# A planned attention and two-MoE kernel: GpSimd's elementwise work kept clear of its maxima, lower parts on VectorE, and q transfers issued closer together

## The chip, the cores and the metric

The kernel runs on one core of a Trainium2 chip. The metric is the device time of one execution, in microseconds. The engines are named as the profile names them: PE (TensorE; PEld its weight loads), DVE (VectorE), ACT (ScalarE), POOL (GpSimd), SP (SyncE, whose queue issues almost every transfer).

## What is computed

The reference, cut to what matters (batch 8, 8 heads, 576 positions, head size 64; all float32):

```
q_s = softmax(q, axis=-1)                      # over the 64 features
k_s = softmax(k, axis=2)                       # over the 576 positions
attn = q_s @ (k_s^T @ v)                       # per batch and head
x  = attn as [4608 tokens, 512]
x  = (silu(x @ w_gate) * (x @ w_val)) @ w_out              # d_ff 1536
out = max(x @ w1, x @ w2, x @ w3) @ w_out2                 # d_ff 768
```

## The kernel before

**Tiles and stages.** The 4608 tokens are nine blocks of 512. Each float32 operand of a product is split into a higher part, rounded to float32r, and a lower part, the rest; each product is three matmuls (high by high, high by low, low by high). Blocks 0, 1 and 2 are stages of their own. Blocks 3 and 4, 5 and 6, 7 and 8 are handled as **pairs**: the two blocks are the halves of a Strassen-Winograd scheme with seven products in place of eight (`wino_unit`, operands `b11`, `t1`, `t3`, `t2`, `b21`, `b22`, `t4`). In the trace the first pair fills about 560 to 910 us, the second 910 to 1240, the third the rest.

**Factors in the first pair.** In the pairs' products the weights' side needs seven factors for each piece of a weight. Three are the weights' own quarters; the other four are sums made earlier and kept in memory. In the first pair these four are read again (`twos_load`, line 626), split (`wino_hi`, line 634, the higher part on ACT; `wino_lo`, line 638, the lower part as sum minus higher part) and stored for the later pairs (`wino_store`, line 647). There are 84 such lower parts. `make_job` (line 1196 on) plans them. Later pairs only read the factors (line 653).

**Attention for later blocks** runs between the products as three chains of steps. The k chain (`k_steps`) loads k, takes the maximum over positions on DVE, then over partitions on POOL (`k_max_all`, line 195: `partition_all_reduce`), subtracts it (`k_sub`, lines 204 and 209), takes the exponential on ACT (line 218) and multiplies with v on PE (line 270). Two q chains (`q_steps`) each handle one half (four heads) of a block's q: loads of q (line 156, eight or sixteen transfers a half), maximum, subtraction (line 237), exponential (243), sum, multiplication by the reciprocal (256), transpose (410), split (414, 418) and the product with k and v (433 to 435, output `px`). One q chain, called `own`, has the second half of the heads and buffers of its own (`qown`). Six maxima on POOL are taken during pairs: four in the first pair, two in the second.

**What sets the order.** Nothing is scheduled by hand or by the framework. A planner written in the kernel walks a list of products and keeps for each engine a list of planned busy stretches with fixed costs. `gap` finds the first free stretch, `do` books it, `best` books whichever engine would end first, and `at` puts the instruction into a heap by planned time. Each engine then runs its instructions in the order of planned time, and what waits for what follows from the data. So a change of one cost or one booking moves work between engines and reorders everything behind it. GpSimd takes elementwise work only in pairs (`alone` is false there). The planner books a maximum as 1.4 us on POOL, an elementwise half tile on POOL as 0.85 us (`HALF`), and knows no time to go from one to the other:

```
            elif e == "B":
                ch["t"] = best(ch["t"], {"D": dur, "G": 2.0 * dur}, fn)
            ...
            else:
                ch["t"] = do(e[0], ch["t"], dur, fn)
```

In the built program POOL has an instruction of its own, shown as `ISA` without tiles, wherever it goes from an elementwise operation to a maximum or back. All transfers of a load step are planned at multiples of a spacing, 1.8 us for q.

Of the kernel before, what the change touches and what calls it, by code (L numbers as in the profile page):

```python
# [21 lines left out]
def linear_attention_moe_moe_kernel(  # L22
# [119 lines left out]
    def q_loads(t, j, hf):  # L142
        hs = slice(hf * HH, (hf + 1) * HH)
        cut = min(D * j, TB)
        todo = []
        for s0, s1 in ((0, cut), (cut, TB)):
            if s0 == s1:
                continue
            b, s = divmod(j * TB + s0, S)
            a = q[b, hs, s:s + s1 - s0, :].rearrange("(g u) (n p) (e i) -> u e g p n i", u=2, p=32, e=2)  # L150
            for u in range(2):
                for e in range(2):
                    p = 64 * u + 32 * e
                    for g in range(HP):
                        todo.append((slice(p, p + 32), g, slice(s0 // 32, s1 // 32), a[u, e, g]))
        return [lambda p=p, g=g, n=n, i=i: nc.sync.dma_start(out=t["qp"][p, g, n], in_=i) for p, g, n, i in todo]  # L156
# [263 lines left out]
    def x_mm(c, j, hf, g, tag):  # L420
        cut = min(D * j, TB)
        if cut == 0 or cut == TB:
            segs = [(0, TB, min(j, B - 1))]
        elif cut <= 256:
            segs = [(0, 256, j - 1), (cut, TB, j)]
        else:
            segs = [(256, TB, j), (0, cut, j - 1)]
        pg = hf * HP + g
        px = ps.tile([128, TB], F32, tag=tag, name="px")
        for a, e, b in segs:  # L430
            hi, lo = kvhi[b % 3][:, pg, :], kvlo[b % 3][:, pg, :]
            qhi, qlo = c["qt"][0][:, a:e], c["qt"][1][:, a:e]
            nc.tensor.matmul(out=px[:, a:e], lhsT=hi, rhs=qhi, start=True, stop=False)  # L433
            nc.tensor.matmul(out=px[:, a:e], lhsT=hi, rhs=qlo, start=False, stop=False)  # L434
            nc.tensor.matmul(out=px[:, a:e], lhsT=lo, rhs=qhi, start=False, stop=True)
        c["px"] = px
# [324 lines left out]
    HALF = {"A": 0.42, "D": 0.43, "G": 0.85}  # L761
    ENG = {"D": nc.vector, "G": nc.gpsimd, "A": None}
    DVE_LATE = 1.0
    KV_WAIT = 3.0
    G_FIRST = False
    LATER = {3: (1, "P", 0), 4: (2, "O", 0)}
# [15 lines left out]
    def at(t, fn, *a):  # L782
        heapq.heappush(events, (t, next(count), fn, a))
# [21 lines left out]
    def best(t, cost, fn, *a, engines="DG", by=0.0):  # L805

        if G_FIRST and not alone[0] and gap("G", t, cost["G"])[0] + cost["G"] < by:
            return do("G", t, cost["G"], fn, *a, nc.gpsimd)
        if alone[0]:
            engines = engines.replace("G", "")  # L810
        e = min(engines, key=lambda e: gap(e, t, cost[e])[0] + cost[e] + (0.4 if e == "G" else 0.0))
        return do(e, t, cost[e], fn, *a, ENG[e])
# [109 lines left out]
    def advance(ch):  # L922
        off = 0.45 * (ch is chains[1]) / 1.8
        while ch["steps"] and ch["steps"][0][0] != "P" and (ch["t"] <= clock[0] + LOOK[len(marks) - 1] or ch.get("bank")):
            e, dur, fn = ch["steps"][0]
            if e == "gate":
                if fn not in gates:
                    return
                ch["t"] = max(ch["t"], gates[fn])
            elif e == "there":  # L930
                there[fn] = ch["t"]
            elif e == "bank":
                bank_free[ch["bank"]] = max(bank_free.get(ch["bank"], 0.0), ch["t"])
                ch["bank"] = None
            elif e == "wait":
                ch["t"] += dur
            elif e == "open":
                gates[fn] = ch["t"]
            elif e == "load":
                t = max(ch["t"], ch.get("last", 0.0))  # L940
                for a in fn[1]:
                    t = (math.ceil(t / dur - off) + off) * dur
                    t = max(t + 0.01, sync(t, a))
                ch["last"] = t
                ch["loaded", fn[0]] = t + 4.5
            elif e == "loaded":
                ch["t"] = max(ch["t"], ch["loaded", fn])
            elif e == "B":
                ch["t"] = best(ch["t"], {"D": dur, "G": 2.0 * dur}, fn)
            elif e in ("D+", "D="):  # L950
                t, ch["i"] = take(ch["t"])
                ch["t"] = do("D", t, dur, fn, ch["i"])
            else:
                ch["t"] = do(e[0], ch["t"], dur, fn)
            if e in ("D-", "D="):
                drop(ch["i"], ch["t"])
            if DEBUG:
                log.append((round(clock[0], 1), chains.index(ch), e, round(ch["t"], 1)))
            ch["steps"].pop(0)
# [56 lines left out]
    def q_steps(runs, ts, direct, gate, own=False, free_q=False):  # L1016

        steps = []

        def load(n):  # L1020
            return "load", 1.8, (n, q_loads(ts[n % len(ts)], *runs[n]))

        for n, (j, hf) in enumerate(runs):
            c, t = {"own": own, "q": int(own)}, ts[n % len(ts)]
            if j in LATER:
                steps.append(("gate", 0.0, ("later", j)))
            if not direct:
                if n == 0:
                    if own:
                        steps.append(("gate", 0.0, gate))  # L1030
                    steps.append(load(0))
                    if own and len(runs) > 1:
                        steps.append(load(1))
                steps.append(("loaded", 0.0, n))
            steps += [
                ("D", 1.22, lambda c=c, t=t: q_max(t, c)), ("D", 0.95, lambda c=c, t=t: q_max_all(t, c)),
                ("B", 1.22, lambda e, c=c, t=t: q_sub(t, c, e)), ("A", 0.65 + 1.3 * direct, lambda c=c, t=t: q_exp(t, c, 0)),
                ("A", 0.65, lambda c=c, t=t: q_exp(t, c, 1)), ("D", 1.22, lambda c=c, t=t: q_sum(t, c)),
                ("D", 1.3, lambda c=c, t=t: q_sum_all(t, c)), ("B", 1.22, lambda e, c=c, t=t: q_mul(t, c, e)),
            ]  # L1040
            for g in range(HP):
                pg = hf * HP + g
                if g == 0 and not direct and not own and n + 1 < len(runs):
                    steps += [load(n + 1)] if free_q else [("gate", 0.0, ("k done",)), load(n + 1)]
                steps += [
                    ("D+", 0.7, lambda i, c=c, t=t, g=g: q_t(t, c, g, i)), ("A", 0.62, lambda c=c: q_t_hi(c)),
                    ("D-", 0.69, lambda c=c: q_t_lo(c)),
                ]
                if g == 0:
                    steps += [("gate", 0.0, ("taken", 2) if j == 4 else gate), ("gate", 0.0, ("kv", min(j, B - 1), hf))]  # L1050
                steps.append(("P", 0.75, lambda bank, c=c, j=j, hf=hf, g=g: x_mm(c, j, hf, g, bank)))
                if direct:
                    steps += [
                        ("A", 0.6, lambda c=c, j=j, pg=pg: x_hi(c["px"], j, pg)),
                        ("D", 0.69, lambda c=c, j=j, pg=pg: x_lo(c["px"], j, pg)), ("bank", 0.0, None),
                    ]
                    if pg % 2:
                        steps.append(("there", 0.0, ("op", f"b{pg // 2 + 1}1")))
                else:
                    steps += [("A", 0.6, lambda c=c, j=j, pg=pg: x_plain_copy(c["px"], j, pg)), ("bank", 0.0, None)]  # L1060
            if own and n + 2 < len(runs):
                steps.append(load(n + 2))
            if not direct:
                steps.append(("open", 0.0, ("x", j, hf)))
        return steps
# [132 lines left out]
    def make_job(use, key, k):  # L1198
        m = [k in t for t in TWOS].index(True)
        if ("two", key, m) not in have or not left("wA"):  # L1200
            return False
        t, o, ks = have["two", key, m]
        t, w = acquire("wA", max(t, use - 9.0))
        t = do("A", t, HALF["A"], wino_hi, key, k, w)
        t = there[key + (k,)] = best(t, HALF, wino_lo, key, k, by=use - 1.5)
        have["w", key + (k,)] = w, sync(max(use, t) + 1.5, wino_store, key, k)
        ks.discard(k)
        have["two", key, m] = max(t, have["two", key, m][0]), o, ks
        if not ks:
            release("or", o, have.pop(("two", key, m))[0])  # L1210
        return True
# [646 lines left out]
```

## Time and profile before

| what | value |
|---|---|
| median of 3 runs | 1563.69 us (1563.63 to 1568.78) |
| the profiled execution, its own time | 1565.22 us |
| its span (first to last instruction) | 1563.2 us |
| mean granted TensorE clock | 0.986 |
| busy: PE, DVE, ACT, POOL | 95%, 66%, 44%, 6% of the span |
| DMA engines | 71% of the span in the main queue |

A span is cut into instructions with the idle time before them and what released them. An engine's instructions run in order, so one that waits holds up all behind it. PE's busy time hides little: its matmuls start about 0.23 us apart when nothing holds them, and what the kernel can lose or gain is the time in which PE waits, and the stretches in which its granted clock is 0.5 in place of 1.0.

### The profile page before, as it was taken

How to read it: one execution, taken by the hardware profiler on the slowest of the kernel's cores; microseconds unless marked ns; L12 is line 12 of the kernel's file. 1: busy time of each engine (PE TensorE's matmuls, PEld its weight loads, DVE VectorE, ACT ScalarE, POOL GpSimd, SP SyncE). 2: the span in 40 equal slices, each digit the busy share in tenths (PEclk: the TensorE clock that was granted, in tenths of full speed). 3: DMA queues.
4: the chain of work that ended last, by engine and by line, in shares of the span. 5: the costliest groups of instructions: out<-in, count | busy, mean ns of one | idle time of the engine just before them, and what ended most of it. 6: DMA issues, size and time to landing. Idle time of an engine off the chain costs nothing.

```text
span 1563.2 us, 20625 instructions
## 1 busy us (share of the span) xinstructions
PE 1480.0 (95%) x6946; PEld 1201.1 (77%) x6946; DVE 1032.7 (66%) x1787; ACT 682.1 (44%) x1184; POOL 100.6 (6%) x86
## 2 busy tenths in 40 slices
PE   3888899999999999989999989999999999999999
PEld 2666687888778887877778877888778788887787
DVE  7879986767777677664478874564587844445553
ACT  3778765544546445544343344233322332224112
POOL 1000000000000001010022130000100300001000
PEclk9999899999999999999999999999999999999999
DMA  7798785974798798877478767774676576646664
GB/s 188 201 318 286 225 245 175 264 229 137 220 291 262 274 317 259 261 223 240 165 211 251 244 211 213 200 205 140 226 205 177 188 228 188 191 152 212 199 193 158
DMA packets 302024, 342.71 MB, mean 219 GB/s; under 512 B 157536, under 2 KB 181088, under 8 KB 301920
## 3 DMA queue, kind: packets, MB, share of 16 engines
q1 hardware_dynamic: 297120, 340.22, 71.2%
q10 hardware_dynamic: 4800, 1.18, 0.4%
q8 instruction: 56, 0.92, 0.2%
q14 instruction: 48, 0.39, 0.1%
HBM read 257.16 MB, written 84.15 MB: 218 GB/s over the span
## 4 chain that ended last, share of the span: by engine, by line
PE 76%; DVE 11%; DMA 6%; issue 3%; ACT 3%; SPq 1%; POOL 0%; DVEq 0%; ACTq 0%
PE pb L668 51%; PE pacc L684 15%; PE pb L684 8%; DMA v_sb<-in_v_dram 1%; PE pkv L270 1%; DMA plain<-raw_V 1%; DVE stage L543 1%; DVE tall L738 1%; DVE hlo L723 1%; DVE wall L567 1%; DMA raw_O<-plain 1%; SPq L156 1%; PE px L434 1%; DMA out_dram<-tall 1%; PE px L433 1%
## 5 line engine op out<-in xcount | busy, mean ns | idle before, releaser
L738 DVE TENSOR_TENSOR tall<-tall,pb 128x512 f32<-128x512 f32 x234 | 159.4, 683 | 195.1 <-PE pb L668 182.8
L668 PE MATMUL pb<-b11h,wall 128*128 128x512 f32 x756 | 267.1, 394 | 8.1 <-ACT s L704 4.6
L668 PE MATMUL pb<-b21h,wall 128*128 128x512 f32 x756 | 263.0, 390 | 0.0
L684 PE MATMUL pacc<-hhi,ow 128*128 128x512 f32 x576 | 191.8, 396 | 7.3 <-ACT hhi L719 6.0
L668 PEld LDWEIGHTS pb<-b11h,wall 128*128 128x128 f32 x756 | 142.3, 189 | 42.4 <-ACT s L704 5.9
L668 PEld LDWEIGHTS pb<-b21h,wall 128*128 128x128 f32 x756 | 141.9, 188 | 30.0 <-ACT tall L728 0.4
L728 ACT COPY tall<-pb 128x512 f32<-128x512 f32 x113 | 66.3, 587 | 203.6 <-PE pb L668 202.7
L668 PE MATMUL pb<-b11l,wall 128*128 128x512 f32 x378 | 147.9, 391 | 0.5 <-DVE b11l L455 0.5
L668 PE MATMUL pb<-b21l,wall 128*128 128x512 f32 x378 | 147.4, 390 | 0.4 <-DVE b21l L455 0.4
L684 PEld LDWEIGHTS pacc<-hhi,ow 128*128 128x128 f32 x576 | 110.0, 191 | 33.3 <-ACT hhi L719 8.6
L719 ACT CAST hhi<-tall 128x512 fp32r<-128x512 f32 x108 | 66.5, 617 | 139.0 <-DVE tall L713 103.6
L684 PE MATMUL pacc<-hlo,ow 128*128 128x512 f32 x288 | 114.7, 398 | 6.6 <-DVE hlo L723 6.6
L567 DVE TENSOR_TENSOR wall<-plain,wall 128x512 fp32r<-128x512 f32 x126 | 86.8, 692 | 43.8 <-ACT wall L564 36.7
L723 DVE TENSOR_TENSOR hlo<-tall,hhi 128x512 fp32r<-128x512 f32 x102 | 71.2, 698 | 52.3 <-ACT hhi L719 51.5
L564 ACT CAST wall<-plain 128x512 fp32r<-128x512 f32 x126 | 77.0, 617 | 64.3 <-DMA plain<-raw_G 14.7
L668 PE MATMUL pb<-b22h,wall 128*128 128x512 f32 x252 | 90.3, 399 | 7.0 <-POOL wall L638 6.0
L684 PE MATMUL pb<-hhi,ow 128*128 128x512 f32 x288 | 91.1, 391 | 1.1 <-DMA ow<-parts_O 0.9
L684 PE MATMUL pacc<-ow,hhi 128*128 128x512 f32 x288 | 89.3, 390 | 2.6 <-DVE ow L584 2.6
L668 PE MATMUL pb<-t4h,wall 128*128 128x512 f32 x252 | 88.7, 393 | 1.9 <-issue 1.9
L668 PE MATMUL pb<-t3h,wall 128*128 128x512 f32 x252 | 88.4, 391 | 2.1 <-DVE tall L738 1.2
L668 PE MATMUL pb<-t1h,wall 128*128 128x512 f32 x252 | 88.8, 393 | 0.0
L668 PE MATMUL pb<-t2h,wall 128*128 128x512 f32 x252 | 88.1, 390 | 0.0
(231 smaller groups left out, 2761.8 us busy)
## 6 DMA issues: line engine op xcount, KB each, us to landing
ow<-parts_O SPq DMA_DIRECT2D x77, 512.0 KB, 4.8
wall<-wino_W SPq DMA_DIRECT2D x153, 256.0 KB, 3.1
wall<-wino_G SPq DMA_DIRECT2D x102, 256.0 KB, 3.1
wall<-wino_V SPq DMA_DIRECT2D x102, 256.0 KB, 3.3
ow<-parts_P SPq DMA_DIRECT2D x32, 512.0 KB, 5.1
wino_W<-wall SPq DMA_DIRECT2D x63, 256.0 KB, 4.0
wino_G<-wall SPq DMA_DIRECT2D x42, 256.0 KB, 3.8
wino_V<-wall SPq DMA_DIRECT2D x42, 256.0 KB, 4.3
```

The lines of the kernel that those rows point to most:

```text
L156: return [lambda p=p, g=g, n=n, i=i: nc.sync.dma_start(out=t["qp"][p, g, n], in_=i) for p, g, n, i in todo]
L270: nc.tensor.matmul(out=c["pkv"][u * D:(u + 1) * D, g, :], lhsT=lhsT, rhs=rhs, start=i == 0, stop=i == R,)
L433: nc.tensor.matmul(out=px[:, a:e], lhsT=hi, rhs=qhi, start=True, stop=False)
L434: nc.tensor.matmul(out=px[:, a:e], lhsT=hi, rhs=qlo, start=False, stop=False)
L564: nc.scalar.copy(out=wall[:, i:i + 2, 0], in_=plain[kind, f].rearrange("p (a n) -> p a n", a=2))
L567: eng.tensor_tensor(out=wall[:, i:i + 2, 1], in0=plain[kind, f].rearrange("p (a n) -> p a n", a=2), in1=wall[:, i:i + 2, 0], op=ALU.subtract,)
L668: nc.tensor.matmul(out=banks[bank], lhsT=a, rhs=b, start=start and n == 0, stop=stop and n == 5, skip_group_check=True,)
L684: nc.tensor.matmul(out=banks[bank], lhsT=lhsT, rhs=rhs, start=first and n == 0, stop=last and n == 2)
L719: nc.scalar.copy(out=hid[key][0], in_=st["h", key[1], key[2], key[3]])
L723: eng.tensor_tensor(out=lo, in0=st.pop(("h", key[1], key[2], key[3])), in1=hi, op=ALU.subtract)
L728: nc.scalar.copy(out=tall[:, i], in_=banks[bank])
L738: eng.tensor_tensor(out=out_, in0=tall[:, x], in1=banks[bank] if isinstance(bank, str) else tall[:, bank], op=ALU.add)
```

## The change

Three edits, all in the planner:

- A maximum on POOL (step "G") is booked with `SWITCH = 8.0` us free on each side of it, so `best` puts no elementwise work of POOL there; it goes to DVE, or to POOL at another time.
- `make_job` plans the 84 lower parts of factors on DVE alone (`MAKE_ON`), where `best` chose between DVE and POOL.
- The transfers of the `own` q chain in the second pair's blocks and later (`runs[0][0] > 4`) are planned 1.0 us apart, not 1.8 (`OWN`).

`X_WAIT` is 0 and changes nothing.

```
+    SWITCH = 8.0
+    X_WAIT = 0.0
+    OWN = 1.0
+    MAKE_ON = "D"
...
+            elif e == "G":
+                t, i = gap("G", ch["t"] - SWITCH, dur + 2 * SWITCH)
+                busy["G"].insert(i, (t, t + dur + 2 * SWITCH))
+                t = max(t + SWITCH, ch["t"])
+                at(t, fn)
+                ch["t"] = t + dur + LAT
...
-            return "load", 1.8, (n, q_loads(ts[n % len(ts)], *runs[n]))
+            return "load", OWN if own and runs[0][0] > 4 else 1.8, (n, q_loads(ts[n % len(ts)], *runs[n]))
...
-        t = there[key + (k,)] = best(t, HALF, wino_lo, key, k, by=use - 1.5)
+        t = there[key + (k,)] = best(t, HALF, wino_lo, key, k, engines=MAKE_ON)
```

Up to the first maximum of the first pair, near 595 us, the two programs' engines have the same order. From there on, three places.

POOL in the first pair, from the second of its four maxima to the fourth; `kb` is the maximum, `k_sb` and `kr_sb` the two parts of k, `wall` the factors, `hlo` the lower part of a hidden tile, `q_sb` a q tile. Before:

```order
L195 ISA kb<-km 128x256
L237 ISA
L237 TENSOR_TENSOR q_sb<-q_sb,qm 128x1024
L638 TENSOR_TENSOR wall<-twos,wall 128x256
L195 ISA
L195 ISA kb<-km 128x256
L638 ISA
L638 TENSOR_TENSOR wall<-twos,wall 128x256
L256 TENSOR_TENSOR q_sb<-q_sb,qs 128x1024
L723 TENSOR_TENSOR hlo<-tall,hhi 128x512
L195 ISA
L195 ISA kb<-km 128x256
```

And now:

```order
L195 ISA kb<-km 128x256
L237 ISA
L237 TENSOR_TENSOR q_sb<-q_sb,qm 128x1024
L195 ISA
L195 ISA kb<-km 128x256
L209 ISA
L209 TENSOR_TENSOR kr_sb<-kr_sb,kb 64x256
L195 ISA
L195 ISA kb<-km 128x256
```

Between two maxima one operation is left on POOL, and no factor's lower part. In all pairs seven `wall`, three subtractions of the large k tile (`k_sb`, line 204) and two `hlo` left POOL for DVE, and one `b11l` came to it; of the q steps as many are on POOL as before, though other ones. The bare `ISA` rows are as many as before, nine in the pairs.

PE at the end of the first pair, where the last product of a q chain (`px`) stands among the last unit's products. Before, behind `t4` and right ahead of the second block's output products (line 684):

```order
L668 MATMUL pb_8070<-t4h,wall 128x512
L433 MATMUL px<-qt,kvhi_66 128x256
L434 MATMUL px<-qt,kvhi_66 128x256
L435 MATMUL px<-qt,kvlo_69 128x256
L433 MATMUL px<-qt,kvhi_68 128x384
L434 MATMUL px<-qt,kvhi_68 128x384
L435 MATMUL px<-qt,kvlo_71 128x384
L684 MATMUL pb_8160<-ow,hhi 128x512 x2
```

And now:

```order
L668 MATMUL pb_8063<-b21h,wall 128x512
L433 MATMUL px<-qt,kvhi_66 128x256
L434 MATMUL px<-qt,kvhi_66 128x256
L435 MATMUL px<-qt,kvlo_69 128x256
L433 MATMUL px<-qt,kvhi_68 128x384
L434 MATMUL px<-qt,kvhi_68 128x384
L435 MATMUL px<-qt,kvlo_71 128x384
L668 MATMUL pb_8073<-b22h,wall 128x512
```

The last q product comes two products of a unit earlier, and the three ahead of it by more.

ACT in the second pair's first unit, behind the fifth maximum; `s<-pb` empties the PSUM bank `b0`, `k_sb` is the exponential of k, and a table load stands wherever the function changes. Before:

```order
L728 COPY tall<-pb_8383 128x512
L704 ACT_TABLE_LOAD
L704 ACTIVATE s<-tall 128x512
L218 ACT_TABLE_LOAD
L218 ACTIVATE k_sb<-k_sb 128x512
L704 ACT_TABLE_LOAD
L704 ACTIVATE s<-pb_8374 128x512
L704 ACTIVATE s<-tall 128x512 x2
L218 ACT_TABLE_LOAD
L218 ACTIVATE k_sb<-k_sb 128x512
```

And now:

```order
L728 COPY tall<-pb_8385 128x512
L218 ACTIVATE k_sb<-k_sb 128x512 x2
L704 ACT_TABLE_LOAD
L704 ACTIVATE s<-tall 128x512
L704 ACTIVATE s<-pb_8374 128x512
L218 ACT_TABLE_LOAD
L218 ACTIVATE kr_sb<-kr_sb 64x256
L704 ACT_TABLE_LOAD
L704 ACTIVATE s<-tall 128x512 x2
```

The exponentials of k went ahead of the unit, and no table load is left between the two `s` that need it first.

## Rows read from the trace of the kernel before

**Rows 1.** The page, part 1: busy us, share of the span, count.

```profile
PE 1480.0 (95%) x6946; PEld 1201.1 (77%) x6946; DVE 1032.7 (66%) x1787; ACT 682.1 (44%) x1184; POOL 100.6 (6%) x86
```

**Rows 2.** Waits of PE, 560 to 1240 us: for whom, us in total, times, longest.

```profile
PE pb L668 <- POOL wall L638: 6.0, 1, 6.0
...
PE px L434 <- DVE qt L418: 2.6, 1, 2.6
PE pkv L270 <- DVE tall L738: 2.1, 2, 1.9
PE pb L668 <- ACT s L704: 1.9, 1, 1.9
PE pacc L684 <- ACT hhi L719: 1.8, 1, 1.8
...
PE pb L668 <- DVE tall L730: 0.9, 1, 0.9
```

**Rows 3.** Stretches: us, busy of PE, PEld, DVE, ACT, POOL; PE's clock; DMA share; GB/s.

```profile
702.20:709.00 6.80, 3.53 (x8) 2.81 (x9) 0.44 (x1) 0.24 (x1) 3.83 (x3) 0.50 0.39 118
760.20:763.60 3.40, 3.40 (x9) 2.65 (x8) 1.39 (x2) 1.76 (x3) 0.00 (x0) 0.51 0.03 5
...
907.00:913.80 6.80, 6.12 (x17) 4.60 (x16) 5.64 (x4) 1.62 (x3) 6.80 (x5) 0.50 0.01 2
947.90:951.30 3.40, 3.40 (x9) 2.67 (x8) 0.69 (x1) 2.24 (x4) 0.00 (x0) 0.50 0.27 77
```

**Rows 4.** Timeline of POOL: start, us, instruction [idle before, and what ended it].

```profile
643.61 1.08 POOL L195 PARTITION_ALL_REDUCE kb<-km  x1 [8.28 <-issue]
...
695.85 1.08 POOL L195 PARTITION_ALL_REDUCE kb<-km  x1 [9.67 <-PE pb L668]
704.70 0.71 POOL L638 TENSOR_TENSOR wall<-twos,wall 128x256 fp32r<-128x256 f32 x1 [7.77 <-issue]
...
755.31 2.37 POOL L204 TENSOR_TENSOR k_sb<-k_sb,kb 128x1024 f32<-128x1024 f32 x1 [6.69 <-issue]
...
929.04 1.08 POOL L195 PARTITION_ALL_REDUCE kb<-km  x1 [7.81 <-DVE km L191]
```

**Rows 5.** Timeline of ACT, two exponentials of k behind a subtraction on POOL.

```profile
606.17 0.63 ACT L218 ACTIVATE k_sb<-k_sb 128x512 f32<-128x512 f32 x1 [3.11 <-POOL k_sb L204]
...
757.71 0.63 ACT L218 ACTIVATE k_sb<-k_sb 128x512 f32<-128x512 f32 x1 [4.73 <-POOL k_sb L204]
```

**Rows 6.** Timeline of DVE and PE at the end of the first pair.

```profile
905.88 0.68 DVE L418 TENSOR_TENSOR qt<-tall,qt 128x512 fp32r<-128x512 f32 x1
...
906.62 0.39 PE L434 MATMUL px<-qt,kvhi 128*128 128x256 f32 x1 [2.63 <-DVE qt L418]
```

**Rows 7.** Timeline of ACT in the second pair's first unit.

```profile
944.48 1.28 ACT L704 ACT_TABLE_LOAD   x1
945.77 0.60 ACT L704 ACTIVATE s<-pb 128x512 f32<-128x512 f32 x1
```

**Rows 8.** DVE: groups of 560 to 1240 us; first pair's stretch; one instruction near 982.

```profile
L638 DVE TENSOR_TENSOR wall<-twos,wall 128x256 fp32r<-128x256 f32 x77 | 38.1, 497 | 10.6 <-ACT wall L634 10.5
L723 DVE TENSOR_TENSOR hlo<-tall,hhi 128x512 fp32r<-128x512 f32 x34 | 24.5, 720 | 29.6 <-ACT hhi L719 29.4
L204 DVE TENSOR_TENSOR k_sb<-k_sb,kb 128x1024 f32<-128x1024 f32 x3 | 3.7, 1226 | 6.8 <-POOL kb L195 6.8
...
560.00:910.00 350.00, 332.60 (x1574) 270.39 (x1573) 242.14 (x443) 153.84 (x289) 42.40 (x31) 0.98 0.76 234
...
981.90 2.93 DVE L713 TENSOR_TENSOR tall<-s,tall 128x512 f32<-128x512 f32 x1
```

**Rows 9.** Timeline of SP's queue: two q loads, the factor load behind them, the last q load.

```profile
809.54 1.01 SPq L156 DMA_DIRECT2D qown<-in_q_dram  x2
...
812.98 0.34 SPq L653 DMA_DIRECT2D wall<-wino_W  x1
...
860.59 0.42 SPq L156 DMA_DIRECT2D qown<-in_q_dram  x1
```

More of the change, by code (lines that the diff above doesn't have):

```diff
@@ L1050, in q_steps @@
                     steps += [("gate", 0.0, ("taken", 2) if j == 4 else gate), ("gate", 0.0, ("kv", min(j, B - 1), hf))]
+                steps += [("wait", X_WAIT * (j > 4), None)] * (not direct)
                 steps.append(("P", 0.75, lambda bank, c=c, j=j, hf=hf, g=g: x_mm(c, j, hf, g, bank)))
```

## The prediction

> **What bounds the kernel now.** The page comes first: PE is busy for 95% of the span and no other engine for more than 77% [rows 1]. So time is gained only where PE waits or where its granted clock is down. The waits of PE in the first two pairs, 560 to 1240 us, come second [rows 2]; the reader is to see that the list is short, that its longest entry, 6.0 us for `wall` of POOL, is a single event, and that the others are single events of 1 to 3 us. Third, the stretches with the granted clock [rows 3]: behind four of these waits PE ran at 0.50, its lower level, for 3.4 or 6.8 us, and each such stretch costs half its length, since PE does in it half of what it does at 1.0. Fourth, the timeline of POOL [rows 4], for the cause: POOL idles for 6.69 to 9.67 us wherever it goes from a maximum to elementwise work or back, although the data are there ("issue" is a wait for nothing that the profile shows). The planner knows nothing of this time. I count it as the bare `ISA` row of the order, a reload of POOL's code.
>
> The Trainium skill says of this, in GPSIMD Engine Reference, section Instruction dispatch, that the first call of a freshly loaded kernel pays about 6 us with no instruction visible. The rows here are longer. By the page's 6 us the first wait below would be an estimated 1.8 us shorter (7.77 less 5.95), and the sum smaller by that; the sum goes by the rows.
>
> **The change, part by part.** The sum is made against the profiled execution, 1565.2 us; the median of the runs is 1.5 us lower.
>
> *Lower parts on DVE only.* At 695.85 POOL took the third maximum, then needed 7.77 us until the lower part of a factor at 704.70 [rows 4]. PE stood 6.0 us for it [rows 2] and then ran 6.8 us at half clock [rows 3]: 6.0 + 3.4 = 9.4 us. With the lower part on DVE no factor waits for POOL. I take all of it. It needs 0.5 us of DVE each [rows 8], seven times.
>
> *No elementwise work near a maximum.* Behind the first and the fourth maximum the subtraction of k was on POOL, and came only after the reload (755.31, idle 6.69 [rows 4]). ACT stood for it 3.11 and 4.73 us at the head of its queue [rows 5], and everything behind it on ACT was late: the splits that PE wants. Behind the fourth maximum PE waited 1.8 us for `hhi` and ran 3.4 us at half clock: 1.8 + 1.7 = 3.5 us. Behind the first it waited 0.9 and 1.9 us for work of DVE that hung on ACT (the entry of 2.1 us has two waits, the longer 1.9 [rows 2]): 2.8 us. On DVE the subtraction takes 1.23 us [rows 8] and follows the maximum at once. I take all 6.3 us. A third such subtraction, in the second pair, held no PE wait of this list, and counts nothing.
>
> *The reloads that stay.* Nine are left, each now with 8 us planned on either side. The rows give 6.69 to 9.67 us for one, so 8 us is about what it takes, not more. What covers the excess: behind a reload stand a q subtraction or a small k part, which are not due within microseconds, and ahead of the maxima the chain of k, whose product is due tens of microseconds later. Without that cover each excess of up to 1.7 us (9.67 less 8) would be a wait of DVE, since the subtraction there now waits for the maximum in DVE's order, and everything behind it.
>
> *ACT behind the fifth maximum.* There PE waited 1.9 us for `s`, which empties a PSUM bank, and ran 3.4 us at half clock: 1.9 + 1.7 = 3.6 us [rows 2, 3]. ACT had the exponential of k between two table loads of 1.28 us right ahead of that `s` [rows 7]. The new order has the exponentials earlier and no load there. The maximum itself ends at 930.1 [rows 4], early enough. I take all 3.6 us, with less trust: it rests on an order that the edits only stir.
>
> *q transfers closer.* At the end of the first pair PE waited 2.6 us for the last `qt` of DVE, done at 906.56 [rows 6], and ran 6.8 us at half clock: 2.6 + 3.4 = 6.0 us [rows 2, 3]. Sixteen transfers at 1.0 in place of 1.8 us end 12.8 us earlier in the plan, and the chain behind them with its steps moves up; PE's last q product now stands two products of a unit earlier and needs `qt` at about 900, 6.6 us earlier than it came. I take the 6.0 us. In the second pair PE hardly waits for q, so the same edit counts nothing there. The price is SP's: a q load holds its queue for about 0.5 us (two in 1.01 [rows 9]), and the factor loads behind it move by that. SP stood idle from 810.55 to 812.98 for a free place in any case [rows 9], which covers the four or five loads that move ahead of it.
>
> *What it costs.* DVE gets 7 x 0.50 + 3 x 1.23 + 2 x 0.72 = 8.6 us more and loses one split: about 8 us, in a stretch where it was busy 242.1 of 350 us [rows 8]. Below, none of it is heard by PE; above, all of it, with two stretches of 3.4 us at half clock, 11 us. DVE is idle for nearly a third of that stretch, so the value is nearer the lower end; but a plan stirred from 595 us on also meets new small waits, as the old one had. I take 5 us.
>
> Sum: 9.4 + 3.5 + 2.8 + 3.6 + 6.0 = 25.3 off, 5 on, 20.3 less than 1565.2: 1544.9, and by the median 1543.4. I forecast **1543 us**. Its own range, with all gained and nothing paid at one end and 11 us paid and the ACT term missing at the other, is 1538 to 1553.
>
> **The rivals.**
>
> *The waits move to DVE.* What left POOL queues on DVE, in order: a subtraction that waits for a late maximum holds all behind it. For it: before, the three subtractions on DVE already waited 6.8 us for POOL in all [rows 8]. The trace also shows DVE held by POOL: an instruction that takes 0.69 us elsewhere took 2.93 at 981.90, while POOL subtracted in the same time [rows 8]. Against: POOL has eleven operations fewer in pairs. Then the last two terms fail, and 6 us are paid: 1563.7 - 15.7 + 6 = 1554. The Trainium skill has the mechanism in SBUF — State Buffer, section Who interferes with whom: a DVE instruction with two inputs in SBUF and a GpSimd instruction that reads SBUF exclude each other for the whole instruction. By that rule the subtractions and lower parts that now run on DVE are of the blocked kind, and it speaks for this rival; the row at 981.90 agrees.
>
> *No change.* PE's wait of 6.0 us also let DVE, ACT and the transfers catch up. Take it away and the next late thing stands in its place, the second pair's start as before. For it: behind each of these waits the engines were ahead for a while. Against: between these five places PE ran for tens of microseconds without a wait of the list. If three quarters of the 25.3 come back: 1563.7 - 25.3 + 19 = 1557 and more, about 1559.
>
> *Slower: q loads hold up factor loads.* One mechanism, in SP's queue: sixteen q loads of 0.5 us close together hold the queue for 8 us; a factor load behind them lands late, PE stands for it and its clock falls. There are four such bursts, two in each of the first two pairs. Each can cost up to 8 us less the 2.4 us for which SP waited anyway [rows 9], plus 3.4 for the clock: 9.0 us. With the ACT and q terms gone, the others are worth 15.7 us, so it decides from three bursts on that are heard in full: 27 - 15.7 = 11 us, 1575. Against: the q loads are still interleaved with factor loads, and the last of them stood behind waiting factor loads up to 860.59 [rows 9], so the old spacing did not spare the queue either.
>
> **How the numbers follow.** Forecast 0.64, waits on DVE 0.19, no change 0.11, slower 0.06. A measurement of this kernel can tell about 0.5%, 7.8 us: faster is below 1555.9. The forecast lies below it, and of the first rival three quarters (0.14): faster 0.78. Same is the rest of that rival and the second one, 0.05 + 0.11 = 0.16. Slower 0.06. The range goes from 1535, a little below the forecast's end, since waits outside the list could fall away too, to 1560, where the second rival ends; it leaves out the slower case and the tails, under 0.2.
>
> **What would show it.** In the changed profile: no wait of PE for POOL `wall`, and no lower part of a factor on POOL; granted clock 1.0 where it was down near 702 and 760; no wait of ACT for POOL `k_sb`; PE without a wait of over 1 us for `qt` at the end of the first pair; one table load fewer in the second pair's first unit. The idle times of POOL ahead of its nine reloaded instructions stay at 7 to 10 us or more and nobody waits for their end. The forecast is wrong if the list of PE's waits in 560 to 1240 us is as long as before with other names, above all DVE `tall` or `wall`, or if PE or its weight loads wait for transfers of factors in 800 to 860 us.

## The result and the profile after

| what | before | after |
|---|---|---|
| median | 1565.33 us (1563.63 to 1568.78, 4 runs) | 1548.93 us (1545.54 to 1549.71, 4 runs) |
| ratio, 95% interval | | 0.9882 [0.9865, 0.9899] |
| profiled execution, its span | 1565.22, 1563.2 us | 1549.41, 1547.6 us |
| mean granted clock | 0.986 | 0.991 |

The change makes the kernel 1.2% faster. The forecast was 1543 us, in a range of 1535 to 1560. Below, a ratio is turned into microseconds by 1565.3.

The page of after, part 1 (answers to [rows 1]):

```profile
PE 1473.2 (95%) x6946; PEld 1196.8 (77%) x6946; DVE 1039.7 (67%) x1796; ACT 680.6 (44%) x1184; POOL 87.6 (6%) x75
```

The waits of PE in after, 560 to 1240 us, the first seven entries (answers to [rows 2]):

```profile
PE pb L668 <- DVE tall L738: 4.0, 4, 1.2
PE pb L684 <- DVE hlo L723: 3.5, 4, 1.6
PE pb L668 <- DVE t2l L455: 2.8, 2, 2.3
PE pacc L684 <- DVE hlo L723: 1.9, 1, 1.9
PE pb L684 <- ACT hhi L719: 1.9, 3, 0.9
PE pb L684 <- DVE tall L738: 1.6, 2, 1.2
PE pb L668 <- issue: 0.9, 1, 0.9
```

The waits at the five places that the prediction named are gone. But the entries for `hlo`, `hhi` and `tall` are longer or new. The whole list adds up to 23.7 us before and to 17.3 now. These two sums are not of the same work, though: the changed kernel is some 15 us further on at 1240 us, so its list ends with waits at the third pair's start, which before stand behind 1240 us (after, 1224 to 1240 us):

```profile
PE pb L684 <- DVE hlo L723: 2.0, 2, 1.6
PE pb L684 <- ACT hhi L719: 0.9, 1, 0.9
```

Another 1.9 us (`pacc` for `hlo`, at 592.70) lie ahead of the first maximum, where both programs have the same order. To compare the same work, take two products of PE: those of lines 668 and 684, 6102 of them, come in the same order in every run of this case. Between the product that starts at 590 us before and the one that starts at 1240, PE's waits fell from 23.6 to 12.6 us, by 11.0 and not by the 15.1 us of the five places.

The rest of the gain is the clock. Stretches of after in the form of [rows 3]: where the third and the fourth maximum stood, and the only stretch at half clock that is left in the first two pairs; behind them the one of before that [rows 3] leave out:

```profile
700.00:710.00 10.00, 10.00 (x46) 8.29 (x45) 3.90 (x7) 9.34 (x14) 0.73 (x1) 1.00 0.80 247
752.00:762.00 10.00, 10.00 (x45) 8.02 (x44) 4.97 (x8) 6.32 (x11) 0.00 (x0) 1.00 0.51 174
793.60:797.00 3.40, 3.40 (x9) 2.69 (x9) 3.40 (x7) 0.00 (x0) 0.00 (x0) 0.53 0.45 122
```

```profile
804.60:808.00 3.40, 3.40 (x9) 2.30 (x8) 3.37 (x6) 0.00 (x0) 0.08 (x1) 0.51 0.48 146
```

Before had 23.8 us at half clock between 560 and 1240 us, after has 3.4. PE is busy for 19.9 of the 23.8, because two of the stretches hold idle time (behind `wall` PE is busy for 3.53 of 6.80 us [rows 3]), and for all of the 3.4: half of the 16.5 that are gone is 8.2 us. With the 11.0 us of waits that is 19.2, and the same work takes 18.4 us less. The two executions as a whole differ by 15.8, because this one of after is 3.9 us late before any edit acts, as the first maximum shows, of before and then of after:

```profile
594.87 1.10 POOL L195 PARTITION_ALL_REDUCE kb<-km  x1 [92.76 <-DVE km L191]
```

```profile
598.80 1.10 POOL L195 PARTITION_ALL_REDUCE kb<-km  x1 [93.89 <-DVE km L191]
```

POOL in after, around the third and the fifth maximum (answers to [rows 4]):

```profile
689.84 1.08 POOL L195 PARTITION_ALL_REDUCE kb<-km  x1 [8.96 <-DVE qs L253]
701.92 0.73 POOL L209 TENSOR_TENSOR kr_sb<-kr_sb,kb 64x256 f32<-64x256 f32 x1 [11.00 <-issue]
...
919.03 1.08 POOL L195 PARTITION_ALL_REDUCE kb<-km  x1 [9.76 <-DVE km L191]
```

The idle times that the prediction counts as reloads are still there, up to 11.00 us, but what comes behind them is wanted by nobody soon. ACT in after, behind the fifth maximum (answers to [rows 7]), and PE's last q product in the first pair (answers to [rows 6]):

```profile
926.14 1.15 ACT L218 ACTIVATE k_sb<-k_sb 128x512 f32<-128x512 f32 x2
927.31 1.28 ACT L704 ACT_TABLE_LOAD   x1
929.78 0.63 ACT L704 ACTIVATE s<-tall 128x512 f32<-128x512 f32 x1 [1.19 <-DVE tall L738]
930.32 0.58 ACT L704 ACTIVATE s<-pb 128x512 f32<-128x512 f32 x1
```

```profile
884.71 0.34 PE L433 MATMUL px<-qt,kvhi 128*128 128x384 f32 x1
```

No table load stands between the two `s`, and the q product waits for nothing. So each place looks as predicted, and yet a part of the gain is missing.

### The profile page after: what moved, and what is told of

It reads as the page before. It is cut to its first block, busy times and chain, and to the rows that moved or that the text cites. A ratio compares the mean times of both kernels' runs of the same rounds, so it can differ in the third digit from the quotient of the medians.

```text
span 1547.6 us, 20610 instructions
## 1 busy us (share of the span) xinstructions
PE 1473.2 (95%) x6946; PEld 1196.8 (77%) x6946; DVE 1039.7 (67%) x1796; ACT 680.6 (44%) x1184; POOL 87.6 (6%) x75
## 4 chain that ended last, share of the span: by engine, by line
PE 75%; DVE 11%; DMA 6%; ACT 3%; issue 3%; SPq 2%; DVEq 0%; ACTq 0%
PE pb L668 50%; PE pacc L684 14%; PE pb L684 8%; DVE hlo L723 1%; DMA ow<-parts_O 1%; PE pkv L270 1%; DMA stage<-in_moe_w_out_dram 1%; DVE stage L543 1%; DVE wall L567 1%; DVE tall L738 1%; SPq L156 1%; DMA v_sb<-in_v_dram 1%; DMA twos<-sums_G 1%; SPq L140 1%; DVE qx L225 1%
## 5 line engine op out<-in xcount | busy, mean ns | idle before, releaser
L738 DVE TENSOR_TENSOR tall<-tall,pb 128x512 f32<-128x512 f32 x234 | 159.6, 683 | 187.7 <-PE pb L668 183.7
L723 DVE TENSOR_TENSOR hlo<-h,hhi 128x512 fp32r<-128x512 f32 x54 | 39.2, 729 | 74.3 <-ACT hhi L719 74.3
```

The costliest lines, as they stand in the source:

```text
L723: eng.tensor_tensor(out=lo, in0=st.pop(("h", key[1], key[2], key[3])), in1=hi, op=ALU.subtract)
L738: eng.tensor_tensor(out=out_, in0=tall[:, x], in1=banks[bank] if isinstance(bank, str) else tall[:, bank], op=ALU.add)
```

## Experiments

A plan that is stirred moves everything behind it, so one edit alone says little about one wait. Several experiments are therefore **swaps**: the planner books and orders as it did, and only the engine that issues an instruction is another. PE's and ACT's orders then stay the same, row for row.

**swap_lo: the seven lower parts on DVE, nothing else.**

```
-        eng.tensor_tensor(out=w[:, 1], in0=two_of(key, k), in1=w[:, 0], op=ALU.subtract)
+        nc.vector.tensor_tensor(out=w[:, 1], in0=two_of(key, k), in1=w[:, 0], op=ALU.subtract)
```

> The kernel before, its plan untouched: every lower part of a factor that the plan gives to POOL is issued on DVE instead, at the same place in the order. PE's and ACT's orders are those of before, row for row; DVE has seven instructions of about 0.5 us more. My theory (the wait of 6.0 us for POOL's reload and the 3.4 us for the clock behind it are lost time, 9.4 us): PE's wait for POOL wall is gone, the granted clock near 702 is 1.0, and the time falls by 9.4 us less at most 3.5 us for DVE's work, from 1565.3 to 1556 to 1559. Rival, no change: what PE waited for let the other engines catch up, the next late thing stands in its place within some 10 us, and the time stays at 1562 to 1565. Rival, the waits move to DVE: PE waits for DVE wall instead, and of the 9.4 us less than half is left, 1561 or more.

Measured: 0.9951 [0.9934, 0.9967], 7.7 us less than before. The wait of 6.0 us is gone and the clock stays up where it had fallen, here in the form of [rows 3]:

```profile
690.00:705.00 15.00, 14.70 (x65) 11.83 (x64) 13.99 (x26) 4.22 (x7) 4.35 (x3) 1.00 0.77 232
```

The waits for `qt` (2.6 us), `s` (1.9) and `hhi` (2.2) are still there. So PE's long wait was lost time, and hardly anything filled its place.

**swap_lo_k: also the large subtraction of k on DVE.**

```
     def k_sub(t, c, part, eng):
+        eng = nc.vector if part == 0 else eng
```

> As the run before it in this list, and also the large subtraction of k is always on DVE, again at its old place in the order. My theory (behind the first and the fourth maximum ACT's wait for POOL's subtraction made PE's waits for hhi, pkv and their stretch at half clock, 6.3 us): another 6.3 us less at most 3.7 us for DVE's three subtractions of 1.23 us; 1549.6 to 1553 in all. PE's wait for ACT hhi near 757 and ACT's two waits for POOL k_sb are gone. Rival, the waits move to DVE: DVE waits in its order for the maximum, what stands behind the subtraction is late, and the time is that of the run before it or more. Rival, no change: 1560 to 1565, other waits of the same size in the same stretches.

Measured: 0.9907 [0.9887, 0.9927], 14.6 us less than before, 6.9 more than the run ahead of it (with an interval of about 4 us to either side). The wait for `hhi` near 757 is gone, and the clock there stays up. The two reload terms are confirmed, without any new plan.

**only_switch: the clearance alone.**

```
+            elif e == "G":
+                t, i = gap("G", ch["t"] - SWITCH, dur + 2 * SWITCH)
+                busy["G"].insert(i, (t, t + dur + 2 * SWITCH))
...
```

> The kernel before with the 8 us of clearance around each maximum alone; lower parts of factors may still go to POOL, and q transfers are 1.8 us apart. In its order no lower part of a factor stands right behind the third maximum and no subtraction of the large k tile is on POOL behind the first and the fourth. My theory: the two reload waits and ACT's waits behind them go by this edit alone, 9.4 + 6.3 = 15.7 us, with 5 us paid about 1554.6 (1550 to 1557); the waits at the end of the first pair (qt) and for s behind the fifth maximum stay. If the lower parts on DVE are needed for the 9.4 us, it is 1559 or more. Rival, each new plan is a draw of its own: new waits of several us in places that this edit doesn't speak of, and a time off these numbers by 5 us or more to either side.

Measured: 0.9893 [0.9877, 0.9909], 16.7 us less. The clearance alone gives nearly all that the change gives, more than expected, since hardly anything is paid. The waits for `qt` (2.6) and `s` (1.9) are there.

**only_own: close q transfers alone.**

```
-            return "load", 1.8, (n, q_loads(ts[n % len(ts)], *runs[n]))
+            return "load", 1.0 if own and runs[0][0] > 4 else 1.8, (n, q_loads(ts[n % len(ts)], *runs[n]))
```

> The kernel before with the own chain's q transfers 1.0 us apart alone. Its order has the last q product two products of a unit earlier and, behind the fifth maximum, the exponentials of k ahead of the unit, so that no table load stands right ahead of s. My theory: the terms at the end of the first pair (6.0 us) and behind the fifth maximum (3.6 us) both go by this edit alone, 9.6 us, with nothing paid on DVE: 1555.7 (1554 to 1559). PE's wait of 6.0 us for POOL wall and its stretch at half clock stay. Rival, the q loads hold up the factor loads in SP's queue: PE or its weight loads wait for transfers in 800 to 870 us, and the time is 1565 or more. If the two terms hang on the other edits, the time stays within 3 us of before.

Measured: 0.9999 [0.9985, 1.0013], a miss: the waits for `qt` and `s` did go and SP held up no factor, and yet nothing was gained. (The third case has the number, but not the reason.) PE's waits in this kernel, 560 to 1240 us, the first two entries:

```profile
PE pb L668 <- POOL wall L638: 5.0, 1, 5.0
PE pb L684 <- DVE hlo L723: 4.5, 3, 3.0
```

`hlo`, which the second block's output products need, is new: 3.0 us at 925, and behind it PE ran at half clock from 927 to 934 us. DVE is what PE waits for, and DVE was full: the first stretch below is 905 to 930 us of this run, the second the same stretch of the run own_swap_ops, told next (columns as in [rows 3]).

```profile
905.00:930.00 25.00, 20.54 (x85) 16.02 (x84) 24.21 (x26) 13.33 (x25) 16.18 (x10) 0.94 0.77 247
```

```profile
905.00:930.00 25.00, 23.86 (x105) 19.33 (x104) 22.91 (x39) 14.53 (x26) 1.09 (x1) 1.00 0.76 251
```

In only_own DVE is busy for 24.21 of 25 us with 26 instructions; where POOL has nothing but one maximum, it does 39 in 22.91.

**own_swap_ops: only_own with the operands of the pairs made on DVE.**

```
-        eng.tensor_tensor(out=tall[:, i], in0=a(), in1=b(), op=ALU.subtract)
+        nc.vector.tensor_tensor(out=tall[:, i], in0=a(), in1=b(), op=ALU.subtract)
...
-        eng.tensor_tensor(out=opnd[op][1][:, c], in0=a, in1=opnd[op][0][:, c], op=ALU.subtract)
+        nc.vector.tensor_tensor(out=opnd[op][1][:, c], in0=a, in1=opnd[op][0][:, c], op=ALU.subtract)
```

> The kernel before with the third edit alone, as run already (0.9999), and now what makes the pairs' operands (differences and lower parts of t1, t2, t3, t4, b11, b21, b22) is always on DVE, at its old place in the order; PE's and ACT's orders are those of the run with the third edit alone. There POOL made operands from 907 to 926 us, and DVE's instructions beside it took up to 1.78 us where they take 0.68 elsewhere: about 9 us in all in that stretch. Theory: POOL's operands cost DVE this time, and that makes hlo late, for which PE waited 4.5 + 2.2 us and ran at half clock behind it. With them on DVE its instructions take 0.7 us, eight or nine more of them are 6 us, so hlo comes some 3 us earlier: the waits for hlo near 924 fall below 1 us, and the time falls by 4 to 8 us, to a ratio of 0.995 to 0.9975. Rival: DVE has too much to do there whoever makes the operands; then the waits for hlo stay or grow and the ratio is 1.000 or more.

Measured: 0.9899 [0.9882, 0.9916], 15.7 us less than only_own, twice what was expected. DVE's groups in 905 to 930 us (busy us, mean ns of one), of only_own, then of own_swap_ops:

```profile
L723 DVE TENSOR_TENSOR hlo<-h,hhi 128x512 fp32r<-128x512 f32 x4 | 4.8, 1225 | 0.0
...
L455 DVE TENSOR_TENSOR t1l<-tall,t1h 128x512 fp32r<-128x512 f32 x2 | 2.4, 1224 | 0.0
...
L738 DVE TENSOR_TENSOR tall<-tall,pb 128x512 f32<-128x512 f32 x2 | 1.4, 677 | 0.0
```

```profile
L723 DVE TENSOR_TENSOR hlo<-h,hhi 128x512 fp32r<-128x512 f32 x4 | 2.7, 684 | 0.0
L1427 DVE TENSOR_TENSOR tall<-xr,tall 128x512 f32<-128x512 f32 x4 | 2.7, 684 | 0.0
...
L455 DVE TENSOR_TENSOR t1l<-tall,t1h 128x512 fp32r<-128x512 f32 x2 | 1.4, 684 | 0.0
```

The same `hlo` takes 684 ns in place of 1225. (The 1225 is a mean of two that run beside POOL, at some 1.75 us each, and two that don't, at 0.68.) Over the whole program DVE has 29 instructions more and is busy for less (1024.8 us after 1033.7); part 1 of the two pages:

```profile
PE 1478.1 (95%) x6946; PEld 1199.6 (77%) x6946; DVE 1033.7 (66%) x1781; ACT 680.9 (44%) x1185; POOL 104.7 (7%) x89
```

```profile
PE 1473.4 (95%) x6946; PEld 1198.5 (77%) x6946; DVE 1024.8 (66%) x1810; ACT 681.7 (44%) x1185; POOL 59.2 (4%) x60
```

So POOL's help with the operands was no help to DVE. That PE has its wait of 4.9 us for POOL `wall` here as well shows that this is another loss than the reloads.

**after_swap_ops and after_swap_all: the same swap in the changed kernel, and a swap of everything.** The first has the edit above; the second is one word:

```
-    ENG = {"D": nc.vector, "G": nc.gpsimd, "A": None}
+    ENG = {"D": nc.vector, "G": nc.vector, "A": None}
```

> The changed kernel with all of the pairs' operands on DVE, at their old places in the order, PE's and ACT's orders as they were. The changed kernel waits for hlo and hhi near 910 to 915 (2.6 us in all), for t2l at 790 (2.3 us and 1.7 for the clock), and DVE's instructions beside POOL's are long there too. Theory (POOL's operands cost DVE more than they save): these waits shrink, 2 to 5 us less than the changed kernel, a ratio of 0.985 to 0.987. Rival (DVE has too much to do): 0.989 or more, with longer waits for DVE in the second and third pair.

> The changed kernel with every elementwise instruction of POOL on DVE, in the same plan and order; POOL has the maxima alone and reloads nothing in the pairs. Theory: a subtraction or multiplication of q on POOL holds DVE's two-input instructions beside it, too, so these also cost DVE about what they take from it: within 2 us of the run with the operands alone on DVE, a ratio of 0.984 to 0.988. Rival: q's steps of 1.23 us each on DVE, in an order that has them between lower parts that PE wants soon, make new waits of 1 us or more: 0.989 to 0.993.

Measured: 0.9807 [0.9787, 0.9828] and 0.9809 [0.9790, 0.9827]: 11.7 and 11.4 us less than the changed kernel, medians 1538.83 and 1538.06 us. Both are faster than the two kernels of this case. The gain is more than twice the expected 2 to 5 us. PE's waits in after_swap_ops, first three entries:

```profile
PE pb L668 <- DVE tall L738: 4.0, 4, 1.2
PE pb L684 <- DVE hlo L723: 2.2, 2, 1.4
PE px L433 <- DVE tall L738: 1.8, 1, 1.8
```

For the same work as above (590 to 1240 us of before) PE's waits are 8.8 us after 12.6, and no stretch at half clock is left in the pairs. What stays on POOL in the first of the two, the q steps, five `hlo` and a small part of k, costs nothing that can be measured.

**no_own_swap_all: is the third edit worth its terms where POOL holds nothing?** after_swap_all with `OWN = 1.8`.

> The changed kernel with all of POOL's elementwise work on DVE, as run already (0.9809), and the own chain's q transfers 1.8 us apart again. It differs from that run by the third edit alone, where POOL holds nothing. Theory (the third edit's two terms are real, and were given back because POOL's operands at the start of the second pair slow DVE): without POOL there the edit is worth its 6.0 + 3.6 us, and this run is at 0.9809 + 0.0061 = 0.987, with PE's waits of 2.6 us for qt and 1.9 us for s and half clock behind them. Rival (whatever PE is spared there is needed by DVE in any case): the edit is worth 0 to 2 us, 0.981 to 0.982, or the two waits are not there.

Measured: 0.9863 [0.9839, 0.9886], 8.5 us slower than after_swap_all (with an interval of about 5 us to either side), where 9.6 was expected. PE's waits have the two again:

```profile
PE px L434 <- DVE qt L418: 2.6, 1, 2.6
...
PE pb L668 <- ACT s L704: 1.9, 1, 1.9
```

**after_no_own: and where POOL makes operands?** The changed kernel with `OWN = 1.8`.

> The changed kernel with the own chain's q transfers 1.8 us apart again: clearance and lower parts on DVE, without the third edit. By the prediction's terms for the third edit (6.0 us at the end of the first pair, 3.6 us behind the fifth maximum) it is 9.6 us slower than the changed kernel: a ratio to the kernel before of 0.9882 + 0.0061 = 0.994. My theory now, from the run with the third edit alone, which gained nothing although both waits went: what PE is spared there it waits for DVE's hlo in the second block's output products, and the edit is worth 0 to 3 us; a ratio of 0.988 to 0.990, with the waits for qt and s back in the trace (2.6 and 1.9 us) and those for hlo near 912 to 915 gone. It also says whether lower parts on DVE add to the clearance, which alone gave 0.9893: not by this theory.

Measured: 0.9900 [0.9881, 0.9918]. The third edit is worth 2.8 us here, with an interval (the two runs' intervals added in squares) of about 4 us to either side. The waits for `qt` and `s` are back as expected, and `hlo`, for which after stood 0.8 and 0.7 us in the second block's output products, holds PE for 0.5 us in all.

**before_swap_all: the kernel before, with the one word.**

> The kernel before, its plan and order untouched, with every elementwise instruction of POOL issued on DVE at its old place. No reload is left in the pairs and nothing holds DVE. Theory: it loses the reload terms (15.7 us) and what POOL's operands cost DVE (11.8 us between the changed kernel and the one with its operands on DVE), 27.5 us in all, and keeps the waits for qt and s: a ratio of 0.9824, faster than the changed kernel (0.9882) although it has none of its three edits. Rival (the clearance and the new plan matter by themselves): 0.986 or more, with new waits for DVE behind the maxima, where its subtractions now stand in the middle of a plan that did not give DVE the time.

Measured: 0.9872 [0.9852, 0.9892], level with the changed kernel, which has all three edits. It is 7.5 us slower than the expected 0.9824: I had added the 11.8 us to a plan in which PE stands for `qt` and `s` at the same place. Where the q product is late, the swap is worth some 5 us, and not 11 to 16 (table below).

**after_no_pool: the planner told so.** `best` drops POOL always, not only outside pairs.

```
-        if alone[0]:
+        if True:
             engines = engines.replace("G", "")
```

> The changed kernel with the planner told that POOL takes no elementwise work in the pairs either, so that DVE's time for it is booked. Theory: as the run in which all of it was moved without a new plan (0.9809), and a little better, since no two jobs are booked on DVE at once: 0.977 to 0.981. Rival (each new plan meets its own small waits, several of 1 to 2 us): 0.982 to 0.986.

Measured: 0.9869 [0.9849, 0.9889]; the theory missed, and the rival (0.982 to 0.986) came nearer. Not several small waits make it, but mainly one place. In this plan the last q product stands at the first pair's end again, in spite of `OWN = 1.0`, and PE waits there:

```profile
PE px L433 <- ACT qt L414: 3.4, 1, 3.4
```

PE also waits 2.3 us for `hlo` at the third pair's start; the wait for `s` is not there in this plan.

**after_no_make: lower parts free to go to POOL again.**

```
-        t = there[key + (k,)] = best(t, HALF, wino_lo, key, k, engines=MAKE_ON)
+        t = there[key + (k,)] = best(t, HALF, wino_lo, key, k, by=use - 1.5)
```

> The changed kernel with the planner free again to give lower parts of factors to POOL: clearance and close q transfers, without the second edit. Five lower parts are on POOL, none between the third maximum and the fourth. By the prediction, which put 9.4 us down to the second edit, it is at 0.9882 + 0.006 = 0.994. My theory now, from the clearance alone (0.9893) and clearance with lower parts on DVE (0.990): the clearance removes the wait for POOL wall by itself and the second edit adds nothing, 0.987 to 0.990, with no wait of PE for POOL wall of over 1 us.

Measured: 0.9906 [0.9890, 0.9922], just outside. No wait for POOL `wall` is left, as expected: the clearance does that alone. But the q product is back at its old place here too, and PE waits for `qt` (2.6 us) and `s` (1.9). The difference to the changed kernel is 3.8 us, with an interval of about 4 to either side. If the second edit adds anything, it is that in the new plan the third one takes effect.

All runs in one table, by three things that can be read in each trace:

| reload waits (PE for `wall`, `hhi`) | last q product early | operands made by | ratio |
|---|---|---|---|
| there | no | POOL | 1 (before) |
| there | yes | POOL | 0.9999 (only_own) |
| there | yes | DVE | 0.9899 (own_swap_ops) |
| gone | no | POOL | 0.9893, 0.9900, 0.9906, 0.9907 (only_switch, after_no_own, after_no_make, swap_lo_k) |
| gone | yes | POOL | 0.9882 (after) |
| gone | no | DVE | 0.9863, 0.9869, 0.9872 (no_own_swap_all, after_no_pool, before_swap_all) |
| gone | yes | DVE | 0.9807, 0.9809 (after_swap_ops, after_swap_all) |

Plans that differ in hundreds of rows agree to 0.15% once these three are the same. By the means of the lower rows the early q product is worth 3.1 us where POOL makes the operands and 9.4 where DVE does. Of the runs under DVE, only own_swap_ops and after_swap_ops moved the operands alone, the others all of POOL's elementwise work; after_swap_ops and after_swap_all, which differ in just that, agree. (swap_lo has half of the reload waits and is left out.)

## Why the prediction was right, and where it was not

The total is right in sign and close in size: 20.3 us forecast, 16.4 by the medians, 18.5 by the ratio. That it is so close is partly luck: two of its terms were wrong, by about the same amount, and offset each other. Each term can be read at its place, since PE's products come in the same order in every run. The table gives the time between the same two products, less that of before, in us, from one execution of each run. The first column is where the stretch lies in before.

| stretch, and what stands there | swap_lo_k | only_own | after_no_own | after | after_swap_ops |
|---|---|---|---|---|---|
| 590 to 640, first maximum | -2.8 | +1.3 | -3.2 | -3.2 | -3.2 |
| 690 to 712, third maximum | -6.8 | -0.2 | -6.8 | -7.1 | -7.0 |
| 745 to 765, fourth maximum | -3.9 | -1.3 | -4.0 | -3.9 | -3.9 |
| 830 to 916, last q products | 0.0 | -4.7 | -0.8 | -3.8 | -5.2 |
| 916 to 935, second block's output products | -0.4 | +7.3 | +1.1 | +3.1 | +1.5 |
| 935 to 956, fifth maximum, `s` | -1.5 | -5.0 | -2.1 | -5.0 | -5.0 |
| 1240 to 1300, third pair's start | 0.0 | 0.0 | 0.0 | 0.0 | -3.3 |
| 590 to the end | -14.5 | -0.8 | -15.9 | -19.5 | -28.2 |

(only_own's +1.3 in the first row is a stretch of 3.4 us at half clock at 616, which before doesn't have.)

- **Lower parts on DVE, 9.4 us:** 7.7 measured by the swap (5.2 to 10.3), 7.3 at the place. The mechanism is right; the sum counts some time twice. The half clock began while PE still stood for `wall`: of the 6.80 us PE was busy for 3.53 [rows 3], so the clock cost 1.8 and not 3.4, and 6.0 + 1.8 is 7.8. That it takes the second edit was wrong: the clearance alone keeps lower parts away from the third maximum.
- **No elementwise work near a maximum, 6.3 us:** 6.9 measured, 6.7 at the two places. Right; ACT's waits were the cause, as said.
- **What it costs, "I take 5 us":** too much. Both swaps together gain 14.6 us, and their terms, with the 7.8, promise 14.1, so nothing that can be measured is paid for work moved to DVE: DVE's idle third covers it, the lower end of the bounds that were given. What the changed kernel pays, it pays at the next term.
- **The term of the q transfers, "I take the 6.0 us":** this is the step that failed. The wait for `qt` went away exactly as said, and the place got 3.8 us shorter in the change, 4.7 in only_own. But right behind it 3.1 and 7.3 us came back, as waits for `hlo` and `hhi` of the second block and, in only_own, as half clock behind them: of the 6.0 us the change keeps 0.7, and only_own loses 2.7. Only where POOL makes no operands do 3.8 stay (after_swap_ops, over both rows). The prediction asked what is late next in SP's queue. What is late next is DVE: right behind that place POOL makes the second pair's operands, and DVE's instructions with two inputs in SBUF take up to 2.6 times as long beside it (1.77 after 0.68 us). PE had been waiting long enough for this not to be seen: with the late q product the two rows together come to 0.3 us where POOL makes the operands (after_no_own) and to 0.0 where DVE does (no_own_swap_all). The row for it was in the trace of before (the 2.93 us instruction of [rows 8]).
- **ACT behind the fifth maximum, "I take all 3.6 us":** it came. The stretch is 5.0 us shorter in after, in only_own too, and 2.9 of these need the third edit (after_no_own has 2.1 without it). The doubt was in place: it does rest on the order, as after_no_make has the third edit and the wait for `s` all the same. The 1.7 us for the clock in this term were not tied to the wait: six of the runs have the wait of 1.9 us without half clock behind it. By the kernel's time both terms together are worth 2.8 us in the change, nothing alone, and 8.5 where POOL makes no operands.
- **The reloads that stay:** right; they took up to 11.00 us, longer than the 9.67 before, and PE's list names none.
- **Rivals.** "The waits move to DVE" had the right mechanism in the wrong place. I priced it for the work that the change moves to DVE; that work is cheap there. What costs is the work that stays on POOL. "No change" fell in size, but what it says of the second pair's start, that the next late thing stands in the place of the wait, is what happened to the q term. The slower case (SP) fell: PE has no wait for a factor's transfer, and only_own, with the same close q loads, is not slower.

By the Trainium skill (SBUF — State Buffer, section Who interferes with whom) a DVE instruction with two inputs in SBUF and a GpSimd instruction that reads SBUF exclude each other, and a DVE instruction with at most one input in SBUF, outside the modes that use both ports, does not take part. The groups above agree: `hlo` 1225 against 684 ns, and L738, which reads one input from PSUM, 677 ns beside a busy POOL. That the one is held up for the other's whole length, as the prediction has it, the section says only of those modes; for two inputs in SBUF it is the row at 981.90 that speaks for it, 2.93 us beside an instruction of POOL that takes 2.39 (`k_sb`, line 204, from 981.89).

The operand swap moves all operands at once. By the table its gain in the changed kernel (28.2 less 19.5, 8.7 us) is 3.0 us from 830 to 935 us, where the second pair starts, 3.3 at the third pair's start, and the rest in smaller pieces elsewhere. Left open: whether another clearance than 8 us would do as well, which wasn't tried.

## What to carry to other kernels

When a wait of the bounding engine is taken away, price what the other engines did during that wait, above all in the microseconds right behind it: if one of them is full there, the gain is only lent. Work given to a helper engine is worth it only if the helped engine's own instructions keep their length beside it, so compare the mean of one form with and without the helper before counting the help. And in a planned kernel, test a cost by swapping the engine of an instruction at its old place, which leaves the plan alone.

## What the hardware showed that was not expected

On instructions with two inputs in SBUF, POOL and DVE together are slower than DVE alone. POOL in only_own, near 923 us, and DVE just before and in the same time (start, us, instruction):

```profile
920.59 1.47 POOL L1427 TENSOR_TENSOR tall<-xr,tall 128x512 f32<-128x512 f32 x1
922.03 1.73 POOL L455 TENSOR_TENSOR b21l<-xr,b21h 128x512 fp32r<-128x512 f32 x1
923.72 3.40 POOL L1427 TENSOR_TENSOR tall<-xr,tall 128x512 f32<-128x512 f32 x2
```

```profile
916.06 0.68 DVE L455 TENSOR_TENSOR t1l<-tall,t1h 128x512 fp32r<-128x512 f32 x1
916.66 0.68 DVE L723 TENSOR_TENSOR hlo<-h,hhi 128x512 fp32r<-128x512 f32 x1
...
920.84 3.46 DVE L723 TENSOR_TENSOR hlo<-h,hhi 128x512 fp32r<-128x512 f32 x2
924.23 1.77 DVE L455 TENSOR_TENSOR t2l<-tall,t2h 128x512 fp32r<-128x512 f32 x1
925.92 1.75 DVE L455 TENSOR_TENSOR b21l<-xr,b21h 128x512 fp32r<-128x512 f32 x1
```

At 916 us POOL is idle, and DVE starts one such instruction every 0.60 us. From 920.59 to 927.67 each engine does four, some 1.7 us apart: eight in 7.1 us, for which DVE alone, at 0.60 each, would need an estimated 4.8. And the idle time of POOL between a maximum and elementwise work, where the profile names no other wait ("issue"), was 5.97 us (only_own, ahead of the maximum at 933) to 11.00 us in these traces.
